# A gate on TensorE before the next QK, with new filler thresholds and a new place for VectorE's tiles, in an attention and GEGLU kernel

## The chip, the cores and the metric

The kernel runs on one core of one Trainium2 chip. The metric is the device time of one execution in microseconds (us); most executions of a kernel agree within 0.3%. Engines are named as in the profile: PE is TensorE's matmuls, PEld its weight loads, DVE is VectorE, ACT is ScalarE.

## The reference, cut to what matters

```python
# x: (1, 2048, 640) bf16, 32 heads of 20, Dff = 1728
h  = x + attention(layernorm(x)) @ wo      # softmax over 2048 keys in each head
h2 = h + (gelu(ln(h) @ w_gate) * (ln(h) @ w_up)) @ w_down
```

Attention needs 32 x 2048 x 2048 exponentials. The kernel cuts them into 2048 tiles of 128 keys by 512 queries (or the same area in another shape).

## The kernel before

The program is laid out at build time. `Sched` holds a table of operations with planned durations and plays them through a list scheduler. The chip then executes each engine's list in that fixed order, with semaphores. So the planner's figures set the order, and the chip sets the time.

```python
MODE_SWITCH = {"pe": .098, "act": 1.28}
...
                if chosen is None:                       # TensorE would have nothing to do
                    if e == "pe" and self.warm is not None:
                        ...
                        if sum(x for _, x in recent) < WARM_MIN * WARM_WIN and (free7 or live):
                            ...                          # issue zeros or one warm matmul by themselves
                o = chosen
                if e == "pe" and self.pad is not None and o.tag and o.tag[0] == "O":   # a PV
                    ...
                    want = PAD_END if o.i in self.final else PAD_MIN
                    while u < want * PAD_WIN and o.util < 1.1:
                        o.fns = o.fns + self.pad         # zeros behind the PV
                        o.dur += 0.215
```

QK stands for the matmuls that make a tile's scores, PV for those that multiply its probabilities by the values. There are two ways for zero matmuls, filler without a result, to come in: behind a PV, and alone when nothing else can start.

A **unit** is one exp on ACT over three PSUM banks (0 to 2) or two (3 and 4), in turn. Its QK fills the banks with one matmul per tile in 32 rows of the array: row group `j`, the head's place in its group of four. Eight tiles in a **slot** of 64 get their exponential from DVE instead. Such a tile's QK is issued after the QK of some unit `u`, directly behind it (158 of 250 in the order of before) or with other work between, and the planner gives it 0.08 us:

```python
        for n, x in dplan:          # n: the unit where the tile has its place, x: the tile (slot, g, kb, j)
            u = max(n - (D_LEAD if slots[x[0]][0] else D_LEAD0), u, D_FIRST, ...)
            dtile[u] = x            # some six units early
            u += 1
...
            qk = op("pe", fns, 0.215, P_QK, mode="row", ...)
            xd = dtile[u]
            if xd:
                qd = op("pe", [qk_mms(lambda: bank(bd), xd, kk) for kk in ...], 0.08, P_QK + 0.5, mode="row", ..., after=[qk])
```

Probabilities stay in 18 tile buffers until PV (column mode, four tiles to a quad, two quads to an operation) has read them. PV of a whole slot accumulates in one PSUM bank.

## Time and profile before

| | before |
|---|---|
| median (4 runs) | 928.62 us |
| span of the profiled run | 926.0 us |
| first exp starts | 35.4 us |
| last exp starts to end of the kernel | 33.7 us |
| exps | 719 |
| zero matmuls recorded | 1048 |

The measure used in this document is the start of one exp minus the start of the exp before, less the floor of 1.330 us (after a three-bank exp) or 0.903 us (after a two-bank exp). **Lateness** is the sum of such excesses of up to 0.6 us after two-bank exps, and a **long wait** is one of over 0.6 us after any exp. Before has 14.9 us of lateness and 1.5 us of long waits. Together with excess after three-bank exps, which is small, this is what a better order could recover. (The prediction's 16.5 us is the sum after two-bank exps, the 1.5 us included.)

### The profile page before, as it was taken

The numbers are of one execution on the slowest core, as the hardware profiler recorded it, in microseconds if no ns is written. First come the engines' busy times: TensorE is split into PE (matmuls) and PEld (weight loads), VectorE is DVE, ScalarE is ACT, GpSimd is POOL, SyncE is SP. The second block draws the span as 40 slices with busy tenths as digits, with TensorE's granted clock in tenths as the row PEclk, the third lists the DMA queues.
The fourth block names the chain that finished last, engine by engine and source line by source line (L and its number), as shares of the span: only waits on it lengthen the run. The fifth ranks groups of instructions, "written<-read, shape, count | busy, mean of one in ns | idle before, by whom it ended". The sixth has DMA issues, their size and how long they took to land.

```text
span 926.0 us, 24582 instructions
## 1 busy us (share of the span) xinstructions
PE 878.1 (95%) x10739; PEld 399.4 (43%) x10771; DVE 812.3 (88%) x1712; ACT 890.2 (96%) x801; POOL 68.2 (7%) x243
## 2 busy tenths in 40 slices
PE   3999999999999999999899999999999999999988
PEld 2432232222232434333244445544544454566667
DVE  8959999999799999888899997989998988989853
ACT  7899999999999999999999999999999999999982
POOL 5000000000024000000042000003020000200100
PEclk9999999999999999999999999999999999999999
DMA  7211010322802000001011000010010000100000
GB/s 257 84 29 49 23 45 27 86 66 66 296 25 23 8 1 1 1 16 43 1 30 30 1 2 8 8 31 23 23 16 16 30 2 16 32 17 9 11 17 16
DMA packets 39523, 34.45 MB, mean 37 GB/s; under 512 B 19436, under 2 KB 36936, under 8 KB 39416
## 3 DMA queue, kind: packets, MB, share of 16 engines
q1 hardware_dynamic: 39416, 32.89, 12.6%
q8 instruction: 84, 1.38, 0.6%
q14 instruction: 23, 0.19, 0.1%
HBM read 20.12 MB, written 8.09 MB: 30 GB/s over the span
## 4 chain that ended last, share of the span: by engine, by line
ACT 47%; PE 45%; DVE 4%; DMA 1%; POOL 1%; issue 1%; SPq 0%
ACT pts L340 30%; ACT rege L340 16%; PE ps L860 14%; PE ps L1056 10%; PE ps L340 10%; PE ps L1117 6%; PE ps L619 4%; DMA regw<-in_A_wqkv_dram 1%; DVE qt_all L340 1%; PE ps L978 1%; ACT L340 1%; DVE qt_all L820 1%; PE ps L564 1%; POOL nw L340 1%; DVE rege L1105 0%
## 5 line engine op out<-in xcount | busy, mean ns | idle before, releaser
L340 ACT ACTIVATE pts<-ps 128x1536 bf16<-128x1536 f32 x480 | 564.3, 1302 | 6.5 <-PE ps L860 4.5
L860 PE MATMUL ps<-qt_all,kt_all 32*128 32x256 bf16 (+2 forms) x3584 | 329.7, 288 | 16.2 <-ACT pts L340 6.2
L340 ACT ACTIVATE rege<-ps 128x1536 bf16<-128x1536 f32 x239 | 290.2, 1299 | 0.8
L860 PEld LDWEIGHTS ps<-qt_all,kt_all 32*128 32x128 bf16 x3584 | 109.6, 92 | 226.9 <-ACT pts L340 96.2
L340 DVE TENSOR_TENSOR qt_all<-qt_all 128x1024 bf16<-128x1024 bf16 (+1 forms) x240 | 164.1, 684 | 3.4
L1056 PE MATMUL ps<-rege,regw 128*128 128x256 bf16 (+1 forms) x1260 | 159.2, 262 | 6.7 <-ACT rege L340 4.7
L340 PE MATMUL ps<-pts,v_all 128*21 128x256 bf16 (+2 forms) x2098 | 142.3, 290 | 1.1 <-DVE osb L340 0.9
L820 DVE TENSOR_SCALAR rege<-ps 128x512 int16<-128x512 f32 x154 | 105.8, 687 | 35.9 <-PE ps L860 33.4
L1056 PEld LDWEIGHTS ps<-rege,regw 128*128 128x128 bf16 x1260 | 98.9, 98 | 60.9 <-issue 35.2
L340 DVE TENSOR_SCALAR qt_all<-qt_all 128x1024 bf16<-128x1024 int16 (+1 forms) x288 | 116.0, 418 | 2.0
L340 PE MATMUL ps<-rege,v_all 128*21 128x256 bf16 (+2 forms) x1294 | 113.6, 292 | 0.0
L340 PE MATMUL ps<-kt_all,zer 128*32 128x512 bf16 x1048 | 85.8, 384 | 0.0
L619 PE MATMUL ps<-regw 128*128 128x512 bf16 (+1 forms) x342 | 80.7, 348 | 2.2 <-issue 0.8
L1117 PE MATMUL ps<-regw,rege 128*128 128x320 bf16 x448 | 79.0, 301 | 1.0 <-DVE rege L1105 0.5
L340 PEld LDWEIGHTS ps<-pts,v_all 128*21 128x21 bf16 x2098 | 50.2, 91 | 43.9 <-issue 33.5
L820 DVE TENSOR_SCALAR qt_all<-ps 128x512 int16<-128x512 f32 x96 | 65.8, 686 | 3.5 <-PE ps L860 1.7
L340 DVE TENSOR_SCALAR rege<-rege 128x1024 int16<-128x1024 int16 (+2 forms) x166 | 67.9, 423 | 1.1
L340 DVE TENSOR_TENSOR rege<-rege 128x1024 bf16<-128x1024 bf16 (+3 forms) x103 | 65.8, 646 | 0.9
L1117 PEld LDWEIGHTS ps<-regw,rege 128*128 128x128 bf16 x448 | 36.8, 98 | 32.0 <-issue 17.0
L1105 DVE TENSOR_TENSOR rege<-rege,ps 128x512 bf16<-128x512 bf16 (+1 forms) x53 | 35.9, 678 | 16.7 <-PE ps L1056 16.4
L340 PEld LDWEIGHTS ps<-rege,v_all 128*21 128x21 bf16 x1294 | 39.8, 91 | 22.3 <-issue 16.8
L619 PEld LDWEIGHTS ps<-regw 128*128 128x128 bf16 x360 | 28.9, 98 | 43.5 <-issue 20.3
(95 smaller groups left out, 626.0 us busy)
## 6 DMA issues: line engine op xcount, KB each, us to landing
rege<-in_A_x_dram SPq DMA_DIRECT2D x6, 640.0 KB, 5.2
q_rows<-regw SPq DMA_DIRECT2D x20, 128.0 KB, 1.8
out_dram<-rege SPq DMA_DIRECT2D x16, 160.0 KB, 2.3
regw<-in_B_w_gate_dram SPq DMA_DIRECT2D x1, 2160.0 KB, 8.2
regw<-in_B_w_up_dram SPq DMA_DIRECT2D x1, 2160.0 KB, 13.2
regw<-in_B_w_down_dram SPq DMA_DIRECT2D x1, 2080.0 KB, 19.6
kt_all<-k_rows SPq DMA_DIRECT2D x12, 160.0 KB
qt_all<-q_rows SPq DMA_DIRECT2D x12, 160.0 KB
```

The source lines that it names most:

```text
L340: return lambda eng: getattr(eng, method)(*args, **kwargs)
L564: op("pe", lambda eng, a=a: eng.transpose(bank16(bk, D)[:, 128 * a:128 * a + 128], src[:, a * 128:(a + 1) * 128], ident[:]), 0.055, prio, ...
L619: yield op("pe", lambda eng, l=l, r=r, k=k: eng.matmul(bank(bk, n), l, r, start=(k == 0), stop=(k == len(steps) - 1)), c_mm(n), prio, mode ...
L820: d_ops.append(op("dve", lambda eng: eng.tensor_scalar(v[:, 512 * h:512 * h + 512], bank(b), EXP_MUL, -32000.0, ALU.mult, ALU.max), c_dve( ...
L860: return lambda eng: eng.matmul(out()[:, kk * nq:(kk + 1) * nq], kt_all[32 * j:32 * j + 32, g, kt * 128:(kt + 1) * 128], qt_all[32 * j:32 ...
L978: op("pe", lambda eng, tt=tt: eng.transpose(bank(b2)[:, tt * 128:(tt + 1) * 128], osb[:, s, tt * 128:(tt + 1) * 128], identf[:]), c_mm(128 ...
L1056: op("pe", lambda eng, a=a, f=f, fi=fi: eng.matmul(bank(bk)[:, fi * ns:(fi + 1) * ns], w[:, a, F0[f]:F0[f] + 128], hnT[:, a, 128 * b:128 * ...
L1105: hdone.append(op("dve", lambda eng, bu=bu, fv=fv, w=w: eng.tensor_tensor(fv, fv, bank(bu, w), ALU.mult), c_dve(w), p, reads=[ku] + hkeys( ...
L1117: op("pe", lambda eng, f=f, o=o, hf=hf, bk=bk: eng.matmul(bank(bk, 320), ha_f[:, o:o + 128], wd[:, f, hf * 320:(hf + 1) * 320], start=(f = ...
```

## The change

The intent: nothing on TensorE may start if it would still run when the next QK falls due, and zeros behind a PV stop short of that time. In the same step thresholds of the filler change, and DVE's tiles lose their lead.

```diff
-WARM_WIN, WARM_MIN = 3.4, 0.55
-PAD_WIN, PAD_MIN, PAD_END = 3.4, 0.42, 0.46
-PE_AGE = 1.0
+WARM_WIN, WARM_MIN = 3.4, 0.5
+PAD_WIN, PAD_MIN = 3.4, 0.42
+QK_LEAD = .3
+PE_AGE = 1.5
...
+                    if e == "pe" and due is not None and o.prio[0] > 0 and t < due < t + o.dur + (MODE_SWITCH[e] if mode[e] not in (None, o.mode) else 0):
+                        skipped.append((p, i))
...
-                    while u < want * PAD_WIN and o.util < 1.1:
+                    room = due - t - MODE_SWITCH[e] if due is not None and due > t else 1e9
+                    while u < PAD_MIN * PAD_WIN and o.util < 1.1 and o.dur + 0.215 < room:
...
+                if e == "act":
+                    due = t + o.dur + (0.905 if o.dur > 1.2 else 1.332) - QK_LEAD if o.mode == "exp" else None
...
-D_LAG = 9
+D_LAG = 8
...
-                dplan.append((len(units) - 1, tiles[i]))
+                dtile.append(tiles[i])          # in its place, no lead
...
-                if len(quads) < PV_QUADS and not final and s_ in pv_bank:
+                if len(quads) < PV_QUADS and not final:
...                                              # and no extra quads after D_HOLD
```

More of the change, by code (lines that the diff above doesn't have):

```diff
@@ L107, in schedule @@
         live = False
+        due = None
         total = len(ops)
@@ L126, in schedule @@
                     got = []
+                    if e == "pe" and due is not None and o.prio[0] > 0 and t < due < t + o.dur + (MODE_SWITCH[e] if mode[e] not in (None, o.mode) else 0):
+                        skipped.append((p, i))
+                        if len(skipped) >= 60:
+                            break
+                        continue
                     for bk in o.acq:
@@ L188, in schedule @@
                     u = sum(x for _, x in recent) + o.util
-                    want = PAD_END if o.i in self.final else PAD_MIN
-                    while u < want * PAD_WIN and o.util < 1.1:
+                    room = due - t - MODE_SWITCH[e] if due is not None and due > t else 1e9
+                    while u < PAD_MIN * PAD_WIN and o.util < 1.1 and o.dur + 0.215 < room:
                         o.fns = o.fns + self.pad
@@ L307 @@
 PV_QUADS = 2
-D_LAG = 9
+D_LAG = 8
 PR, PR2 = 12, 6
 ND = 4
-D_PER_SLOT = (8, 8, 8, 8, 8, 8, 8, 8)
+D_PER_SLOT = (8,) * len(SIZES)
 D_SLOT0 = 2
-D_FIRST, D_SPAN, D_LEAD, D_LEAD0, D_HOLD = 1, 16, 6, 4, 4
+D_FIRST, D_SPAN = 1, 16
 RSQRT_MAGIC = float(0x5F3759DF)
@@ L769, in bass_sequential_preLN__mha_block__glu_gated_geglu__prompt_kernel @@
         PAT = [((0, 1, 2), (3, 4))] * len(CHUNKS)
-        units, ubank, dplan, ends = [], [], [], []
+        units, ubank, dtile, ends = [], [], [], []
         i, in_slot = 0, {}
@@ L781, in bass_sequential_preLN__mha_block__glu_gated_geglu__prompt_kernel @@
             want = min(nd, (k[0] - D_FIRST) * nd // D_SPAN + 1) if k[0] >= D_FIRST else 0
-            if k[1] < want and i < len(tiles) and tiles[i][0] == s_:
-                dplan.append((len(units) - 1, tiles[i]))
+            if k[1] < want and tiles[i][0] == s_:
+                dtile.append(tiles[i])
                 k[1] += 1
                 i += 1
+            else:
+                dtile.append(None)
             k[0] += 1
@@ L788, in bass_sequential_preLN__mha_block__glu_gated_geglu__prompt_kernel @@
         assert all(k[1] % 2 == 0 for k in in_slot.values())
-        chunk_u = [min(u for u, tl in enumerate(units) if slots[tl[0][0]][0] == c) for c in range(len(CHUNKS))]
-        dtile = [None] * len(units)
-        u = 0
-        for n, x in dplan:
-            u = max(n - (D_LEAD if slots[x[0]][0] else D_LEAD0), u, D_FIRST, chunk_u[1] if slots[x[0]][0] == 1 else 0)
-            dtile[u] = x
-            u += 1
         d_tiles = set(x for x in dtile if x)
@@ L915, in unit @@
                     for x in list(d_done):
-                        if u - x_unit[x[2]] >= D_LAG and x[2][0] == s_ and x[2][3] not in [y[2][3] for y in have]:
+                        if u - x_unit[x[2]] >= D_LAG and x[2][3] not in [y[2][3] for y in have]:
                             have.append(x)
                             d_done.remove(x)
-                if any(x[2][0] == s_ and u - x_unit[x[2]] >= D_LAG + D_HOLD for x in d_done):
+                while final and d_done:
                     have = []
                     for x in list(d_done):
-                        if x[2][0] == s_ and u - x_unit[x[2]] >= D_LAG and x[2][3] not in [y[2][3] for y in have]:
-                            have.append(x)
-                            d_done.remove(x)
-                    quads.append(have)
-                while final and any(x[2][0] == s_ for x in d_done):
-                    have = []
-                    for x in list(d_done):
-                        if x[2][0] == s_ and x[2][3] not in [y[2][3] for y in have]:
+                        if x[2][3] not in [y[2][3] for y in have]:
                             have.append(x)
@@ L951, in unit @@
                     sc.final.add(pv)
-                    assert not any(x[0] == s_ for x in d_raw)
+                    assert not d_done and not d_raw
                     epilogue(s_, bk)
@@ L957, in base @@
             n = CHUNKS[c][1]
-            if n == 512:
-                return 0
-            half = sum(1 for _, m in CHUNKS[:c] if m == 256) % 2
-            return 2 * half + (n == 128 and CHUNKS[c - 1][1] == 128)
+            if n == 128:
+                return 2 + (c == len(CHUNKS) - 1)
+            return 2 * (c % 2) if n < 512 else 0
         def epilogue(s_, bk):
```

## The prediction

> **What bounds the kernel now.** I read the page's busy table first.
>
> ```profile
> span 926.0 us, 24582 instructions
> PE 878.1 (95%) x10739; PEld 399.4 (43%) x10771; DVE 812.3 (88%) x1712; ACT 890.2 (96%) x801; POOL 68.2 (7%) x243
> ```
>
> ACT and PE both look full, so the busy shares do not say which one sets the pace. The rows of the page's 40 slices and two group lines come next.
>
> ```profile
> PE   3999999999999999999899999999999999999988
> ACT  7899999999999999999999999999999999999982
> PEclk9999999999999999999999999999999999999999
> ...
> L340 ACT ACTIVATE pts<-ps 128x1536 bf16<-128x1536 f32 x480 | 564.3, 1302 | 6.5 <-PE ps L860 4.5
> ...
> L340 PE MATMUL ps<-kt_all,zer 128*32 128x512 bf16 x1048 | 85.8, 384 | 0.0
> ```
>
> PE's 95% contains 1048 zero matmuls, four to a group, that are there only to keep the array active: 262 groups of about 0.215 us (the planner's figure) are some 56 us of filler. PE therefore has room and ACT, with the exponentials, is the pacemaker; the granted clock never drops. ACT's idle time before the exps is tiny (6.5 us, and 0.8 us for those that write `rege`). That number misleads, because neighbouring ACTIVATEs overlap in the records. The groups kept apart by shape show it:
>
> ```profile
> L340 ACT ACTIVATE pts<-ps 128x1536 bf16<-128x1536 f32 x240 | 362.8, 1512 | 6.5 <-PE ps L860 4.5 <-PE ps L340 1.1
> L340 ACT ACTIVATE pts<-ps 128x1024 bf16<-128x1024 f32 x240 | 262.1, 1092 | 0.0
> L340 ACT ACTIVATE rege<-ps 128x1536 bf16<-128x1536 f32 x120 | 181.1, 1509 | 0.8
> L340 ACT ACTIVATE rege<-ps 128x1024 bf16<-128x1024 f32 x119 | 129.5, 1088 | 0.0
> ```
>
> A three-bank exp lasts 1.51 us and a two-bank exp 1.09, 2.60 together, yet in the timeline a pair is over in less. ACT around 500 us, at full pace:
>
> ```profile
> 498.77 2.48 ACT L340 ACTIVATE pts<-ps 128x1536 bf16<-128x1536 f32 x2
> 501.00 2.51 ACT L340 ACTIVATE rege<-ps 128x1536 bf16<-128x1536 f32 x2
> 503.24 4.79 ACT L340 ACTIVATE pts<-ps 128x1536 bf16<-128x1536 f32 x4
> ```
>
> From start to start a pair takes 501.00 - 498.77 = 2.23 and then 2.24 us. So a wait of up to 0.2 us hides inside overlapping records. I therefore took, over the whole trace, the start of each exp minus the start of the exp before. After a three-bank exp the next one starts 1.330 us later at the 5th percentile and 1.336 on average: 2.3 us lost in 358. After a two-bank exp the floor is 0.903 and the mean 0.949: 16.5 us lost in 355. **All that TensorE's order of work can give back is 18.8 us**, 2.0% of the time, nearly all of it where a three-bank QK has to fit beneath a two-bank exp. The timeline shows how one is lost:
>
> ```profile
> 252.75 2.37 ACT L340 ACTIVATE rege<-ps 128x1536 bf16<-128x1536 f32 x2
> ...
> 254.14 0.83 PE L340 MATMUL ps<-kt_all,zer 128*32 128x512 bf16 x12
> ...
> 254.91 0.39 PE L860 MATMUL ps<-qt_all,kt_all 32*128 32x512 bf16 x3
> ...
> 255.34 1.45 ACT L340 ACTIVATE pts<-ps 128x1536 bf16<-128x1536 f32 x1 [0.23 <-PE ps L860]
> ```
>
> Three groups of zeros run from 254.14; QK starts at 254.91 and the exp at 255.34, 2.59 after 252.75 instead of 2.23. Over the trace such a QK costs nothing if it starts up to 0.46 us after the two-bank exp has started; beyond that, every 0.1 us is 0.1 us of ACT. Late by over 0.06 us are 81 of 355. The kind of matmul just before these QKs: zeros 25 times (4.9 us), chains of full-array matmuls 49 times (about 10 us over all such cases), PV four times (0.8 us), others below 0.6 us.
>
> **What the Trainium skill says.** "ScalarE: Activation LUTs", section "What ACT_TABLE_LOAD costs", gives an ACTIVATE with immediate operands 186 ns + 0.833 ns per element and an overlap of about 93 ns back to back: 1373 and 946 ns of spacing for 1536 and 1024 elements. The trace has 1330 and 903, 43 ns less each; the trace decides. "TensorEngine Tiling (Array Packing)", section "Key Properties", says that a change of tiling mode drains TensorE. The trace agrees: from the last start in one mode to the first in another is 0.205 us at the median from full to row mode and 0.311 from column to row. "TensorE: Matmul & The Clock Gate", Part 1, says that the clock halves after an idle window of about 3.4 us; what share of activity suffices it does not say. I summed array time by shape over 3.4 us windows: 1% of them have a share below 0.345, the lowest 0.22, and the clock stayed whole. So somewhat fewer zeros should not cost the clock.
>
> **The change, part by part.**
>
> *The gate.* When an exp starts, `due` becomes its planned end, plus the planned length of the next exp, less 0.3. While a three-bank exp A runs, this is 0.905 - 0.3 = 0.605 us after the start of the two-bank exp B, later than the 0.46 that the chip allows. An operation started before A ends is refused only if it takes more than 0.605. Plain PV is 2 x 0.218 + 0.098 for the switch = 0.534, a full matmul about 0.22 + 0.098: both pass. Only PV with zeros and PV of three quads (0.75) are touched. Also, `due` moves on to the next QK when B starts, while the QK under A's banks is ready only 0.115 + 0.056 = 0.171 later; in that hole a long operation is not stopped, and one refused just before can slip in. A PV with one group of zeros (0.75) hurts if it starts between 0.46 - 0.75 = -0.29 and +0.17 around B's start: 0.29 of that stretch of 0.46 is guarded, to a limit that can still leave some 0.1 us. I count half of the zeros' 4.9 us: **-2.5**. PV: 0.8, half: **-0.4**. The 10 us behind full chains stay: the gate lets them pass.
>
> *Thresholds.* `WARM_MIN` from 0.55 to 0.5 and no `PAD_END` mean fewer zeros. A warm matmul was last before a late QK once, so the worth is near nothing; at the very end a group or two less is about **-0.2**. `PE_AGE` from 1.0 to 1.5 keeps TensorE longer in one mode. Of 1645 changes of mode 197 lie between full and column mode; a third fewer is 65 x 0.2 = 13 us of PE time in 850, 1.5% less backlog, worth perhaps **-0.5** of the 10 us.
>
> *VectorE's tiles without a lead.* Eight of 64 tiles in a slot get their exponential on DVE. They were started six units ahead of their place and are now started in place; the lag until PV falls from 9 to 8 units. ACT's work is unchanged: the same 250 tiles on DVE, the same 719 exps. A slot is 56 / 2.5 = 22.4 units of (1.336 + 0.949) / 2 = 1.14 us, 25.6 us; the last DVE tile comes in unit 15, 8 us before the end. By start-to-start times a pair of tiles costs DVE 2 x 0.60 + 4 x 0.33 + 3 x 0.60 = 4.3 us, so it is ready in time unless DVE is behind by 4. It is then too late for an ordinary quad, and the last PV of a slot gets one or two more quads of 0.22 us: 32 slots x 0.33 = 10 us of PE work, where there is room. That I put at **+0.5**, the last slot, which is bare, at **+0.4**, and a few slots where DVE is behind at **+0.5**.
>
> Sum: -2.5 - 0.4 - 0.2 - 0.5 + 0.5 + 0.4 + 0.5 = -2.2, so 928.9 becomes 926.7.
>
> **Rivals.** *The gate works fully*, and the rest of the lateness goes with it because the planned order changes everywhere: at most 18.8 us, time 910. For it: all late QKs have one form. Against: 10 of the 16.5 us lie behind short matmuls that the gate lets pass, and the planner charges 0.098 for a switch that takes about 0.2, so the chip falls behind its plan whatever the plan is. I would expect 920 as the best. *The lead was worth something*: without it, last PVs wait for DVE, the single PV bank stays occupied, probability buffers run full and ACT stalls at slot ends. For it: DVE is 88% busy over the span and 97% between 100 and 200 us. Against: 18 tile buffers are 7.2 units, some 8 us, of which a batch of PV uses about half, so a PV can be 4 us late for free. With 0.3 us lost in each of 32 slots the time is 937. *The clock halves* in some windows with fewer zeros: one such window of 3.4 us makes three exps late by about 0.2 us, 0.6 us each; ten of them give 933. Against: the windows at 0.22 that kept the clock.
>
> **Range and chances.** The centre is the sum, rounded to 926.5. Downwards 920 is the good case. Upwards the second rival has more room, so 937. Faster by over 2% needs 910.3, the whole hidden idle time: 0.02. Slower by over 2% needs 947.5, 0.6 us in each slot, well beyond the rival: 0.07. Within: 0.91.
>
> **What would show it.** Start-to-start excess after two-bank exps falls from 16.5 to about 13, with the part behind zeros halved and the part behind full chains as it is; fewer than 1048 zero matmuls, perhaps 900; 719 exps; first exp at 35 us as before, and some 32 us from the last exp to the end. Wrong would be: a fall in the part behind full chains, new ACT gaps of over 0.5 us at slot ends with DVE named as releaser, or a granted clock below 1.

## The result, and the profile after

The changed kernel takes 926.08 us (median of 4 runs, 925.17 to 926.13), before 928.62. The ratio is 0.9971, with a 95% interval of 0.9954 to 0.9989. Ratios are the mean time of one kernel's fast runs over that of the other's of the same rounds, so not quite the ratio of the medians quoted. The time is 0.4 us from the predicted 926.5. The page of after begins:

```profile
span 924.3 us, 23924 instructions
PE 844.1 (91%) x10407; PEld 385.6 (42%) x10440; DVE 811.5 (88%) x1712; ACT 886.6 (96%) x801; POOL 70.4 (8%) x243
...
L349 ACT ACTIVATE pts<-ps 128x1536 bf16<-128x1536 f32 x480 | 570.5, 1357 | 9.4 <-PE ps L864 5.7
...
L349 PE MATMUL ps<-kt_all,zer 128*32 128x512 bf16 x728 | 59.8, 384 | 0.0
```

PE is less busy by 34 us, and 320 zeros are gone. ACT's idle time before the exps has risen from 6.5 to 9.4 us and the mean record from 1302 to 1357 ns, although the kernel is faster: both columns point the wrong way. By shape (busy, mean ns, idle before):

```profile
L349 ACT ACTIVATE pts<-ps 128x1536 bf16<-128x1536 f32 x240 | 376.3, 1568 | 9.0 <-PE ps L864 5.7 <-PE ps L349 2.9
L349 ACT ACTIVATE pts<-ps 128x1024 bf16<-128x1024 f32 x240 | 275.0, 1146 | 0.4 <-PE ps L349 0.2
```

Records are longer (1568 against 1512 ns) while the floor from start to start is the same 1.330 us, so a longer record is not more work: neighbours overlap more. Only starts can be compared. They give this account of the spans, in us:

| part | before | after | difference |
|---|---|---|---|
| first exp starts | 35.37 | 36.22 | +0.84 |
| excess after three-bank exps | 2.31 | 3.06 | +0.75 |
| lateness after two-bank exps | 14.94 | 8.88 | -6.06 |
| long waits after two-bank exps | 1.51 | 4.88 | +3.37 |
| interruptions by GELU | 36.52 | 37.22 | +0.70 |
| last exp starts to end | 33.67 | 32.36 | -1.31 |
| sum | | | -1.71 (spans: -1.73) |

So a gain of 6 us and a new cost of 3.4 us hide behind a small difference. One of the new long waits, on ACT, DVE and PE in the timeline of after:

```profile
506.63 2.64 ACT L349 ACTIVATE rege<-ps 128x1536 bf16<-128x1536 f32 x2
508.85 0.42 DVE L349 TENSOR_SCALAR rege<-rege 128x1024 int16<-128x1024 int16 x1
510.28 0.62 PE L349 MATMUL ps<-pts,v_all 128*21 128x256 bf16 x16
511.37 1.45 ACT L349 ACTIVATE pts<-ps 128x1536 bf16<-128x1536 f32 x1 [2.10 <-PE ps L349]
```

ACT stands still for 2.10 us and is released by a PV. It is the last PV of a slot, which must take in the slot's last DVE tiles; the last step of the last pair's exponential (`rege<-rege`, in place) ends at 508.85 + 0.42 = 509.27, and the PV starts a microsecond after. Before had no wait there. A wait of 1.12 us at 269 us is of the same kind. The third, 1.27 us at 844 us, is another matter: it is released by a QK, and the granted clock was 0.5 for 3.4 us from 840.0 us on. The mean clock of after is 0.998 in all four runs; that of before was 1.000 in its profiled run and in every run beside the experiments.

### The profile page after: what moved, and what is told of

The parts are those of the page before. It is cut to its first block, busy times and chain, and to the rows that moved or that the text cites. A ratio compares the mean times of both kernels' runs of the same rounds, so it can differ in the third digit from the quotient of the medians.

```text
span 924.3 us, 23924 instructions
## 1 busy us (share of the span) xinstructions
PE 844.1 (91%) x10407; PEld 385.6 (42%) x10440; DVE 811.5 (88%) x1712; ACT 886.6 (96%) x801; POOL 70.4 (8%) x243
## 4 chain that ended last, share of the span: by engine, by line
ACT 75%; PE 15%; DVE 7%; DMA 2%; SPq 0%; issue 0%; DVEq 0%
ACT pts L349 48%; ACT rege L349 26%; PE ps L1052 4%; PE ps L864 4%; DVE rege L349 3%; PE ps L349 3%; PE ps L628 3%; PE ps L1113 2%; DMA regw<-in_A_wqkv_dram 1%; ACT L349 1%; DVE rege L824 1%; DVE qt_all L349 1%; PE ps L573 1%; DMA rege<-o_nat 0%; SPq L349 0%
## 5 line engine op out<-in xcount | busy, mean ns | idle before, releaser
L349 ACT ACTIVATE pts<-ps 128x1536 bf16<-128x1536 f32 x480 | 570.5, 1357 | 9.4 <-PE ps L864 5.7
L864 PE MATMUL ps<-qt_all,kt_all 32*128 32x256 bf16 (+2 forms) x3584 | 309.6, 289 | 46.6 <-ACT pts L349 30.2
L349 ACT ACTIVATE rege<-ps 128x1536 bf16<-128x1536 f32 x239 | 297.4, 1362 | 0.2 <-PE ps L864 0.2
L864 PEld LDWEIGHTS ps<-qt_all,kt_all 32*128 32x128 bf16 x3584 | 97.7, 92 | 258.4 <-ACT pts L349 140.4
L349 PE MATMUL ps<-pts,v_all 128*21 128x256 bf16 (+2 forms) x2098 | 138.8, 290 | 0.0
L628 PE MATMUL ps<-regw 128*128 128x512 bf16 (+1 forms) x341 | 82.8, 351 | 3.3 <-DVE regw L658 0.9
L349 PE MATMUL ps<-kt_all,zer 128*32 128x512 bf16 x728 | 59.8, 384 | 0.0
L349 PEld LDWEIGHTS ps<-rege,v_all 128*21 128x21 bf16 x1294 | 41.0, 91 | 20.3 <-issue 14.4
L1101 DVE TENSOR_TENSOR rege<-rege,ps 128x512 bf16<-128x512 bf16 (+1 forms) x53 | 35.9, 678 | 15.2 <-PE ps L1052 14.8
## 6 DMA issues: line engine op xcount, KB each, us to landing
regw<-in_B_w_up_dram SPq DMA_DIRECT2D x1, 2160.0 KB, 14.6
```

Of the source, the lines that this page charges most:

```text
L349: return lambda eng: getattr(eng, method)(*args, **kwargs)
L628: yield op("pe", lambda eng, l=l, r=r, k=k: eng.matmul(bank(bk, n), l, r, start=(k == 0), stop=(k == len(steps) - 1)), c_mm(n), prio, mode ...
L864: return lambda eng: eng.matmul(out()[:, kk * nq:(kk + 1) * nq], kt_all[32 * j:32 * j + 32, g, kt * 128:(kt + 1) * 128], qt_all[32 * j:32 ...
L1101: hdone.append(op("dve", lambda eng, bu=bu, fv=fv, w=w: eng.tensor_tensor(fv, fv, bank(bu, w), ALU.mult), c_dve(w), p, reads=[ku] + hkeys( ...
```

## The experiments

Each kernel ran four to six times beside before on the same chip; all are correct. (The runs e1 to e4, e5 to e8 and e9 to e12 were on three chips, so kernels of different groups are compared by their ratios.) In the table, "shared" is the number of DVE tiles (of 250) whose QK uses a row group that its unit's own QK uses as well, counted in the program. The theories are named in the expectations. In the first four of these "lateness" still means the whole sum after two-bank exps, 16.5 us in before; the table and the text after each expectation use the split.

| run | median us | ratio to before | lateness | long waits | last exp to end | shared |
|---|---|---|---|---|---|---|
| before | 928.62 | 1 | 14.9 | 1.5 | 33.7 | 173 |
| after | 926.08 | 0.9971 | 8.9 | 4.9 | 32.4 | 0 |
| e1_gate | 930.21 | 1.0013 | 15.7 | 2.2 | 33.3 | 173 |
| e2_thr | 928.72 | 0.9997 | 12.3 | 0.6 | 36.0 | 173 |
| e3_nolead | 929.09 | 1.0007 | 7.0 | 8.2 | 35.2 | 0 |
| e4_gate_thr | 930.12 | 1.0016 | 14.6 | 2.0 | 34.2 | 173 |
| e5_free | 922.94 | 0.9940 | 11.4 | 1.3 | 31.8 | 0 |
| e6_shared | 936.77 | 1.0094 | 20.3 | 1.7 | 35.9 | 249 |
| e7_pvrules | 935.52 | 1.0097 | 18.5 | 4.2 | 32.8 | 173 |
| e8_free_gate_thr | 921.49 | 0.9924 | 9.4 | 1.2 | 31.1 | 0 |
| e9_after_no_gate | 928.95 | 1.0006 | 7.6 | 9.4 | 32.4 | 0 |
| e10_neutral | 931.18 | 1.0031 | 15.7 | 1.5 | 34.9 | 173 |
| e11_told | 932.39 | 1.0025 | 6.5 | 10.5 | 36.1 | 173 |
| e12_free_few_zeros | 923.36 | 0.9941 | 10.1 | 3.8 | 32.1 | 0 |

### One part at a time

**e1_gate**: before plus the three `due` hunks of the diff above (`QK_LEAD`, the refusal, the limit on zeros), nothing else.

> The kernel before with the gate alone (refusal of long operations and the limit on zeros), thresholds and tile plan untouched. Theory G (the prediction's): the gate stops the zeros from delaying QK. Then the time falls by about 2.9 us to 926, the lateness after two-bank exps from 16.5 to about 13.5, and the part behind zero matmuls from 4.9 to about 2.5. Rival F (fewer zeros did it, whatever the gate does): the order that this kernel issues has 996 zeros instead of 1048, so nearly nothing happens: 928.6 within 1 us, lateness 15 to 17, part behind zeros above 4.

Measured: 930.21 us, lateness 15.7; behind zeros 5.3 us, where before had 5.1. The gate alone does nothing for QK. Nor is it shown to cost time: the one run at a clock of 1.000 took 928.58 us, as before, and the other four, at 0.998, took 929.66 to 930.43. The program shows why it does nothing: of the 288 PV operations of before only three carry zeros. All other zeros are issued alone, when TensorE has nothing to start, and that path the gate does not cover. Built with the limit on zeros alone, the kernel has the same number of zeros and changes of mode as before.

**e2_thr**: the three thresholds alone.

```diff
-WARM_WIN, WARM_MIN = 3.4, 0.55
-PAD_WIN, PAD_MIN, PAD_END = 3.4, 0.42, 0.46
-PE_AGE = 1.0
+WARM_WIN, WARM_MIN = 3.4, 0.5
+PAD_WIN, PAD_MIN, PAD_END = 3.4, 0.42, 0.42
+PE_AGE = 1.5
```

> The kernel before with the thresholds alone (WARM_MIN 0.5, the limit at the slot ends 0.42 instead of 0.46, PE_AGE 1.5), no gate, same tile plan. Theory G: worth 0.7 us, 928, lateness about 16. Rival F: 812 zeros are issued instead of 1048, TensorE falls behind its plan less, the lateness falls to about 11 to 13 and the main phase shortens by 4 us; the time is 924 to 926 if the end of the kernel stays as it is.

Measured: 928.72 us. With 812 zeros lateness falls by 2.6 us, as rival F wanted, and the end takes the gain back: 36.0 us instead of 33.7. The down projection's matmuls from the start of the last exp on, in before and then in e2_thr, show part of the reason:

```profile
L1117 PE MATMUL ps<-regw,rege 128*128 128x320 bf16 x56 | 8.0, 299 | 1.0 <-DVE rege L1105 0.5 <-DVE rege L1081 0.5
```

```profile
L1117 PE MATMUL ps<-regw,rege 128*128 128x320 bf16 x74 | 10.7, 299 | 0.5 <-DVE rege L1081 0.5
```

Eighteen matmuls of the chunk before, 10.7 - 8.0 = 2.7 us, were left over when the last exp began. They had been background work under exps and now lie bare.

**e3_nolead**: before with the tile plan and PV rules of after, without gate and thresholds (the hunks from `D_LAG` on).

> The kernel before with the tile plan of after alone: VectorE's tiles start in their place and not six units ahead. Both theories: slower. The prediction put this part at 1.4 us (930). If the two long stalls that after shows at ends of slots (2.5 and 1.1 us, ACT released by PV) are its price in general, stalls of over 0.6 us sum to some 5 us here and the time is 932 to 936.

Measured: 929.09 us. The long waits came as expected (8.2 us), and the slowdown did not: lateness has halved to 7.0 us. Neither theory had that. The part that I had booked as a cost contains the gain.

**e4_gate_thr**: e1_gate and e2_thr together, that is, after with the lead kept.

> The kernel before with gate and thresholds, the lead of VectorE's tiles kept: after without its tile plan. If the missing lead is what after pays, this is faster than after by its stalls: no waits of over 0.6 us behind PV, lateness about 10, time 922 to 924. Theory G and rival F differ in the distance from the run with thresholds alone: G wants 3 us less here than there, F within 1 us of it.

Measured: 930.12 us, lateness 14.6. Keeping the lead loses the whole gain. Both theories fall: the gain of after needs something that comes with the missing lead.

### A new theory: row groups

Two stretches of before, in the timeline, each a three-tile QK followed by one DVE tile's QK (four matmuls) and then other work:

```profile
201.30 0.39 PE L860 MATMUL ps<-qt_all,kt_all 32*128 32x512 bf16 x4
201.62 0.33 PE L978 MATMUL ps<-identf,osb 128*128 128x128 f32 x1
...
247.44 0.60 PE L860 MATMUL ps<-qt_all,kt_all 32*128 32x512 bf16 x4
247.98 0.40 PE L340 MATMUL ps<-kt_all,zer 128*32 128x512 bf16 x4
```

At 201.30 the unit uses row groups 3, 0 and 1 and the DVE tile 2: all four run at once, and the next operation starts 0.32 us later. At 247.44 the unit uses 1, 2 and 3, and the DVE tile 2 as well: it waits its turn, and the next operation starts after 0.54. Over the trace of before the medians are 0.54 us with a shared row group and 0.33 without, about 0.21 us apart, a whole matmul. The Trainium skill has the principle, in "TensorE: Matmul & The Clock Gate", Part 3, "The mechanism": matmuls overlap when they sit in different row groups.

A tile in its own place follows the unit's tiles in the order of heads, so its row group is always free; six units early it is arbitrary, and 173 of 250 share. I took this for 173 x 0.21 = 36 us of TensorE's time that the planner, with its 0.08 us, does not know of, and the expectations below count in this way. That is too much: only where the tile's QK directly follows its unit's does sharing cost anything, which in the order of before is so for 112 of the 173. 112 x 0.21 = 24 us.

**e5_free**: the lead kept, but only beside units that leave the row group free.

```diff
             u = max(n - (D_LEAD if slots[x[0]][0] else D_LEAD0), u, D_FIRST, ...)
+            while x[3] in [y[3] for y in units[u]]:
+                u += 1
```

> The kernel before, lead kept, but each DVE tile's QK is put beside a unit that does not use its row group (0 of 250 share one, against 173 before). New theory R (row groups): a shared row group makes QK plus the tile's QK take 0.535 us instead of 0.325, which the planner does not know; this backlog made QK late, and the missing lead of after happens to remove it. Then lateness after two-bank exps, waits of over 0.6 us left out, falls from 14.9 to 7 to 9 us, waits of over 0.6 us stay at about 1.5, and the time is about 922 if the end of the kernel stays within 1.5 us. Rival P (the PV rules of after, 32 fewer PV operations, are what helped): lateness stays at 14 to 16, time 928 to 930.

**e6_shared**: the opposite dose.

```diff
+            while u < n - 1 and x[3] not in [y[3] for y in units[u]]:
+                u += 1
```

> The opposite dose: the kernel before with 249 of 250 tiles put beside a unit that does use their row group. Theory R: 76 more times 0.21 us of TensorE's time, lateness of 18 to 20 us, the time 932 or more. Rival P: as before, 15 us, 928 to 930.

Measured: 922.94 and 936.77 us. With 0, 173 and 249 shared row groups (0, 112 and 146 of them in direct succession) the lateness is 11.4, 14.9 and 20.3 us. Both edits shorten the tiles' mean lead, from 5.5 units to 4.1 and 4.9, yet move the time in opposite directions, so the shorter lead cannot explain both. The busy time of all QK matmuls (their number never changes) follows; the page's group line of before, after and then the same line of e5_free and e6_shared:

```profile
L860 PE MATMUL ps<-qt_all,kt_all 32*128 32x256 bf16 (+2 forms) x3584 | 329.7, 288 | 16.2 <-ACT pts L340 6.2
```

```profile
L864 PE MATMUL ps<-qt_all,kt_all 32*128 32x256 bf16 (+2 forms) x3584 | 309.6, 289 | 46.6 <-ACT pts L349 30.2
```

```profile
L862 PE MATMUL ps<-qt_all,kt_all 32*128 32x256 bf16 (+2 forms) x3584 | 311.4, 289 | 27.1 <-ACT pts L340 14.8 <-ACT rege L340 7.8 <-DVE rege L1107 0.5
```

```profile
L862 PE MATMUL ps<-qt_all,kt_all 32*128 32x256 bf16 (+2 forms) x3584 | 341.0, 288 | 14.7 <-ACT pts L340 8.7 <-ACT rege L340 2.6 <-issue 1.0
```

The mean of one matmul stays at 288 to 289 ns; only the overlap changes. From e5_free to e6_shared the busy time grows by 29.6 us, and 146 x 0.21 is 31. In after PE waits 30.2 us for ACT before QK, in before 6.2: TensorE is ahead where it was behind. Theory R had wanted 7 to 9 us of lateness in e5_free; it is 11.4, so row groups are part of the drop to 7.0 in e3_nolead and not all of it.

**e7_pvrules**: the lead kept, PV by the rules of after (`D_LAG` 8, no early single quad, no extra quads after a hold).

> The kernel before with the PV rules of after alone (no early single quad at a slot's start, no extra quads after a hold, lag 8), lead kept, 173 shared row groups: 256 PV operations instead of 288, 60 fewer changes of mode. Rival P: lateness falls to about 8 to 10, as in the run without a lead. Theory R: lateness stays at 13 to 15; some long waits behind last PVs appear, 928 to 932.

Measured: 935.52 us (934.32 to 942.18), lateness 18.5. With 32 PV operations fewer lateness rises. Rival P falls: these rules do not help while the lead is kept. How much they cost is less sure, since no run of this kernel had the full clock: four runs (934.32 to 935.92) were at 0.996 to 0.998 and two (942) at 0.989.

**e8_free_gate_thr**: e5_free with gate and thresholds of after.

> Free row groups with the lead kept, and gate and thresholds of after: meant to beat both kernels. Theory R: lateness 6 to 8, waits of over 0.6 us below 2, 692 zeros; time 919 to 923. If gate and thresholds do nothing, within 1 us of the run with free row groups alone, apart from the end of the kernel.

Measured: 921.49 us (920.69 to 921.98), ratio 0.9924. This beats both kernels: no shared row groups as in after, long waits of 1.2 us as in before. Against e5_free in the same rounds it gains 1.4 us, of which lateness accounts for 1.9; behind zeros it fell from 2.9 to 1.2 us.

### Controls

**e9_after_no_gate**: after with the three `due` hunks taken out.

> The changed kernel with the gate taken out again, thresholds and tile plan of after kept. It issues 776 zeros (after: 728). If the gate matters through QK's lateness, that rises from 8.9 to 11 us or more here. If it acts only as one more reshuffle of the order, lateness is 8 to 10 and the difference from after lies in waits of over 0.6 us and in the end of the kernel, which the planner itself puts 5 us later (915.6 against 910.3): 928 to 932.

Measured: 928.95 us. Lateness is 7.6 us, lower than with the gate; the long waits are 9.4 us, against 4.9. By the ratios (1.0006 against 0.9971, from different rounds) the gate is worth some 3 us in this setting, by the spans of the two profiled runs 1.7, and none of it comes from QK's lateness, which is what the gate is for.

**e10_neutral**: before with one threshold moved by a hair.

```diff
-PE_AGE = 1.0
+PE_AGE = 1.05
```

> A control: the kernel before with PE_AGE 1.05 instead of 1.0, which changes the order of TensorE's operations and nothing of their number apart from seven groups of zeros. What its time differs from before is the size of pure reordering. I expect lateness of 14 to 16 and a time within 2 us of before, on either side; a difference as large as that of after (2.5 us) would mean that one change of a threshold says little about its reason.

Measured: 931.18 us, ratio 1.0031 (0.0031 x 928 = 2.9 us slower), with the same lateness and long waits within 1 us and an end 1.3 us later. Reordering alone, with seven groups of zeros more, moves this kernel by as much as the whole change did.

**e11_told**: the planner knows what a shared row group costs.

```diff
-                qd = op("pe", [...], 0.08,
+                qd = op("pe", [...], 0.293 if xd[3] in [x[3] for x in tl] else 0.08,
```

> The kernel before with 173 shared row groups, but the planner is told 0.293 us for such a tile's QK instead of 0.08. Theory R in its narrow form (the plan's ignorance makes QK late): lateness falls to about 10, time 924 to 927. In its wide form (the 36 us of TensorE's time themselves): lateness stays at 13 to 15 and the end of the kernel comes later as background work is left over, 929 to 933.

Measured: 932.39 us, in two groups: 925.88 and 925.97 at a mean clock of 1.000, and 932.20 to 933.98 at 0.989 to 0.991. The profiled run is one of the latter; its clock was halved for 17 us from 484.5 us on, where four of its long waits (6.0 us) lie. The lateness of 6.5 us and the two runs at full clock speak for the narrow form (knowing the cost repairs the order): lateness is lower than in e5_free although all 173 still share. But two runs are little.

**e12_free_few_zeros**: e8_free_gate_thr with less filler.

```diff
-WARM_WIN, WARM_MIN = 3.4, 0.5
-PAD_WIN, PAD_MIN, PAD_END = 3.4, 0.42, 0.42
+WARM_WIN, WARM_MIN = 3.4, 0.4
+PAD_WIN, PAD_MIN, PAD_END = 3.4, 0.3, 0.3
```

> The best kernel so far (free row groups, gate, thresholds) with 484 zeros instead of 692 (activity aimed at 0.40 and 0.30 instead of 0.50 and 0.42). Rival F in its place: each group of zeros less is backlog less, lateness falls from 9.4 to 7 to 8 us and the time to about 919, if the granted clock stays at 1. If the clock halves in some windows, the time is 925 or more and the clock below 0.99.

Measured: a median of 923.36 us, and again it depends on the clock: 919.28 at 1.000, 920.19 at 0.998, 923.09 to 924.49 at 0.993 to 0.987, 928.30 at 0.985. The stretches of its profiled run (the columns are PE, PEld, DVE, ACT and POOL busy, then the granted clock):

```profile
260.00:310.00 50.00, 42.72 (x358) 13.18 (x352) 48.06 (x110) 48.18 (x43) 17.88 (x56) 0.93 0.10 25
...
480.00:880.00 400.00, 372.15 (x5987) 196.36 (x5981) 361.50 (x748) 399.52 (x348) 38.17 (x142) 1.00 0.08 16
```

With 484 zeros the clock drops in places, and whether it does varies from run to run. The number of zeros alone does not decide it: e7_pvrules (1068) and e11_told (964) also had runs at 0.989. Beside e8_free_gate_thr less filler gains 1.4 to 1.8 us in single runs at the same clock (0.998 and 1.000, on another chip), and against its median of 921.49 us loses 1.6 to 6.8 where the clock drops.

## Why the prediction was right or wrong

**The number was right, and the account of it was not.** The predicted -2.2 us is the sum of three parts, gate, thresholds and tile plan. The gate's has the wrong mechanism, and the other two missed the larger gains and costs of which their effects are made. All three signs of being wrong that the prediction names were seen in after: the part behind full chains fell, ACT had new gaps at slot ends (though PV and not DVE is named as the releaser), and the clock fell below 1.

- *What bounds the kernel.* Right. ACT's 719 exps and their floor of 801.6 us from start to start are the same in every run, and nothing gained more than the 18.8 us named as the most to be had.
- *The gate, -2.9.* Wrong. The step that failed is "Only PV with zeros and PV of three quads (0.75) are touched", followed by "I count half of the zeros' 4.9 us". I took zeros before a late QK to be zeros behind a PV. Three PV operations of 288 carry any; the others come alone. The gate by itself left the part behind zeros at 5.3 us and gained no time (e1_gate). In after that part did fall, from 5.1 to 2.6 us (1.1 of it the long wait at 269 us), but together with the thresholds and the free row groups, and taking the gate out again (e9_after_no_gate) left it at 2.1.
- *"The 10 us behind full chains stay".* Wrong. Without long waits it went from 8.6 to 5.8 us. Those QKs were late because TensorE was behind its plan, and with free row groups it is less so (8.6 to 6.9 us in e5_free alone).
- *What the prediction gives for the backlog.* Misread. "The planner charges 0.098 for a switch that takes about 0.2": the 0.205 us are from start to start and contain the last matmul itself. In the trace of before the next start comes 0.205 us after a 256-column matmul of the full array when the mode changes and 0.109 when it doesn't. The change adds 0.096, and the planner was right. So changes of mode do not put the chip behind its plan, and the 13 us for a third fewer of them would have been 6.
- *Thresholds, -0.7.* Too small in the main phase (lateness fell by 2.6 us in e2_thr) and blind to the end of the kernel, where leftover background work took it back (+2.4 us).
- *The tile plan, +1.4.* The net size was near (+0.7 us by the ratio of e3_nolead), made of parts that I had not seen: -7.9 us of lateness, +6.7 us of long waits, +1.5 us at the end. The claim that failed is that the change leaves TensorE's work alone here but for extra quads. It takes away 24 us of waiting between matmuls that share a row group.
- *Second rival* (the lead was worth something). Its mechanism is real: long waits released by a slot's last PV, 3.6 us of them in after. I had spread it as 0.3 us over each of 32 slots; it hit two.
- *Third rival* (the clock). Real too, once in after: one halved window of 3.4 us and a wait of 1.3 us, where I had estimated 0.6.

That the sum landed 0.4 us from the measurement is luck: the neutral control moved by 2.9 us without any reason that a sum of this kind could hold.

**What is shown and what is open.** Shown: the gate does not lower QK's lateness, neither alone (15.7 us against 14.9), nor with the thresholds (e4_gate_thr 14.6 against e2_thr 12.3), nor in after (8.9 against 7.6 in e9_after_no_gate); a shared row group costs 0.21 us where one QK directly follows the other, and under a plan that does not know it, more of them means more lateness and time (e5_free, before, e6_shared, 13.8 us from end to end, well beyond reordering). Shown for the one trace, by the releaser: the long waits behind last PVs in after. Argued only: that the gate's 3 us in after are mere reshuffling. Open: why lateness falls to 7.0 us without a lead and only to 11.4 with a lead and free row groups, and why the PV rules of after raise it when the lead is kept.

## What to carry to other kernels

When a build-time planner fixes the order, look first for durations in the plan that the chip does not keep; a guard inside the plan cannot prevent a delay that the plan does not contain. Small matmuls that are meant to ride along with others need a row group of their own. And before a gain of 0.3% is explained, change something neutral once: if that moves the time as much, only doses and doubled costs can tell causes apart.

## What the Trainium skill lacked or had wrong

- "TensorE: Matmul & The Clock Gate", Part 3: it says that tiles in different row groups run at once, and puts no figure on a matmul that shares one. The runs: 0.54 us against 0.33 us from a QK to the next operation, one whole 512-column matmul more.
- "TensorEngine Tiling (Array Packing)", "Key Properties": it says that a change of mode drains, without a figure. In the trace of before the next start after a full-array matmul of 256, 320 and 512 columns comes at a median of 0.205, 0.232 and 0.312 us when the mode changes to row, and 0.109, 0.136 and 0.216 us when it stays: the change adds 0.096 us.
- "TensorE: Matmul & The Clock Gate", Part 1: it does not say what share of activity keeps the clock. With filler aimed at 0.50 and 0.42 the clock was 0.998 to 1.000 in e8_free_gate_thr, with 0.40 and 0.30 it was 0.985 to 1.000 in e12_free_few_zeros, differing from run to run; but with the thresholds of before it was 0.989 to 0.998 in e7_pvrules, so the aim of the filler does not settle it. It does state window and halving as seen here: most halved stretches are 3413 ns at 0.5.
- "ScalarE: Activation LUTs", "What ACT_TABLE_LOAD costs": spacing of exps is 43 ns shorter than it gives (1330 and 903 ns). The overlap of records is no constant of 93 ns: the mean record of a three-bank exp is 1512 ns in before and 1568 in after at the same spacing.
